# Windowed attention and a rational feed-forward layer: four early halves divided after their value products

## The chip, the cores and the metric

The kernel runs on one core of a Trainium2 chip. The metric is the device time of one execution, in microseconds (us). The engines meant by the short names of the profile are: PE, the matrix engine (PEld is its weight load); DVE, the vector engine; ACT, the scalar engine; POOL, the GpSimd engine; SP, which here only starts transfers. PE accumulates into PSUM, a small memory of banks of 128x512 float32; the other tiles lie in SBUF.

## What is computed

```python
# q, k, v: (4, 8, 768, 64); block 32, window 16, 24 blocks
k_sum = k.reshape(B, H, nb, block, D).max(axis=3)
v_sum = v.reshape(B, H, nb, block, D).mean(axis=3)
scores_l = where(|i - j| < 16, scale * q @ k.T, -1e9)
scores_s = scale * q @ k_sum.T + log(32)
s = concat([scores_l, scores_s]);  a = exp(s - max(s))
a = a / (sum(a) + 1e-9)
attn = a @ concat([v, v_sum])
# x = attn as (3072 tokens, 512)
h = x @ w_in                                  # 512 -> 2048
P = a0 + a1*h + a2*h**2 + a3*h**3
Q = 1 + |b0|*|h| + |b1|*h**2
out = (P / (Q + 1e-6)) @ w_out                # 2048 -> 512
```

## The kernel before

The 3072 tokens are worked in six groups of 512. A group is eight **halves** of 64 query rows; a half `jj` holds all eight heads, as four pairs. One half sees 96 neighbouring keys and 24 block keys, 120 columns for each pair, so that its scores are a tile of 128 rows by 4 x 120. The feed-forward layer walks over 16 slices of 128 hidden columns for each group; a step is `h0` to `h95` (first layer, 12 matmuls of 128x512), the rational function (`gelu`, named so in the code), and `P3` to `P98` (second layer).

The first 16 halves go through `early_half`. Half by half it is a chain of steps on different engines: DVE takes the maximum of each row of scores; ACT forms the exponentials (`ss`); the row sums give a reciprocal (`sm`); the exponentials are multiplied by it; PE transposes them (`pt`), they are copied to SBUF (`pts`), PE multiplies them with the values (`av`); the result is rounded to `xh`, and DVE forms the rest `xl = av - xh`. Together `xh` and `xl` of eight halves are the input of the first layer: `h0` needs all of halves 0 to 7. `PATH` has a letter for each half. Path `B` subtracts the maximum on DVE, takes one exponential over all four pairs, and sums on DVE. Path `A` multiplies the maximum by the scale on DVE and gives it to ACT as a bias, one exponential for each pair, whose row sum ACT gives as well (an extra instruction, `ACTIVATION_READ_ACCUMULATOR`). The division is four multiplications on POOL, or on DVE for the halves in `SSV`.

The block means of the values of the first batch are made by PE (`vs`, ten times four matmuls that read all value tiles), copied by ACT to half 0's value tile and from there to the seven others (`m0` to `m7`). No `av` can run before its half's means are there.

Weights come packed. `w_split` unpacks a slice in up to six steps, and `MODE` has a letter for each slice: in mode `c` ACT forms the high part and DVE subtracts it from the whole to get the low part (`wearly<-wr,wearly`); in mode `e` ACT forms the high part and its negative, and a DMA started by POOL adds the whole onto it.

The order of all this is written out. `ORDER` is a list of 1,698 tokens; each runs one step of one chain (`a3` is the next step of half 3, `h0` the first-layer matmuls of step 0, `w5` the next step of slice 5), and the class `Kept` ties every instruction of an engine behind the one issued before it. So each engine works strictly in the order of the list. `SLOTS` assigns each tile of a pool to one of its buffers, and a tile waits for the readers of the buffer's last tile. `BYDVE` names the copies that DVE makes in place of ACT: `C` is the copy of a half's transposed tile, `X` its rounding to `xh`.

In the profile all of these instructions stand under line 162, the line of `Kept`; they are told apart by tile names.

Of the kernel before, what the change touches and what calls it, by code (L numbers as in the profile page):

```python
# [51 lines left out]
PATH = 'BAAAAAAAAAAAAABB'  # L52
BYDVE = 'C2 C3 C4 C6 X0 X2 X3'
MEANS = 'aaaggggg'
XP = ()
SSV = (3, 5)
AFF = (28,)
FILL = {}
SLOTS = {'wm': '1010', 'ta': '01101010101010101010101010101010101010101010101010101010101010101010101010101010101010101101010101', 'tq': '01010101010101010101010101101010101011001010101010101101010101010101011010010101010101010010101010', 'st': '010101010101010101010101', 'gh': '012020120120120120120120120120120120120120120120121021021021021021021021020120120120120120120210210210', 'h': '0101011110101010101010101010101010010110100100101010101011010101001010101001001010110010101011010110101100101010100101010', 'ks': '0101', 'o': '01230130213021301320132013201320132013201', 'gl': '0121021021021021021021021021021021021021021021021021021021021021021021021021021021021021012102102102', 'sm': '012302312031203102310213021301230132103210321023', 'p': '0132103210123012301021302020232132302103013201021212131032010213013010121321202301021310101013020301021302130', 'xl': '0101010', 'a': '010010101001010101110010101010010111010000010010010111100001101111010010001010011011101000100010101010010100010101010101010101010', 'tu': '010101010101010101010101010101010101010101010101010101010101010101010101010101010101010101101010101', 'xh': '0110101', 'pts': '010101011011011010101011010101010101011011010101', 'vs': '01'}
NROW = 96  # L60
PTP = 'hhhhhhhhaaaaaaaa'
AVP = 'ooooooooaaaaaaaa'
# [10 lines left out]
h3 W8 a9 g2 g1 q2 a8 a9 A10 h4 a8 w6 W7 g2 w6 g1 g1 w6 o a8 a9 D10 L13 a8 P3 w6 w6 a8 g2 g2 g1 a9 g3 w8 g2 w6 g4 V10 W9 a9 q3 g3 w8 g3 b5 w7 q3 a11 P4
a11 w9 w7 q4 g4 g3 g3 W10 g3 q4 g4 a10 D13 a11 h5 w7 P5 w9 a10 L11 g4 h6 w8 g5 g4 w8 L12 w10 w7 g4 P6 w9 P7 D11 V11 q5 A13 D12 q5 g6 g5 w9 w10 w7 a10
a11 w7 g5 a10 g6 w8 h7 q6 a11 A12 g5 w9 a11 k13 a10 a10 a11 g5 a11 a10 a10 w8 g6 k12 w9 a11 W11 a10 q6 b6 g5 w10 g6 g6 g7 g7 W12 q7 w11 w10 w10 g6 g7
q7 a13 a13 A14 h8 A15 g7 g8 w12 a12 w11 P8 g7 h9 g8 w12 q8 w10 g7 w11 w11 q8 w12 g9 P9 W15 g9 g8 P10 a12 g8 h10 g8 w12 g8 w11 b7 a12 g9 q9 w11 q9 g9
w12 g10 W13 g9 P11 a15 h11 w12 V12 g9 w15 q10 a15 W14 a13 g10 P12 w13 a12 w13 g10 a13 V13 a14 q10 g10 A17 h12 g11 g11 w13 a13 g10 q11 w13 w13 g11 a12
w14 q11 g10 a15 a13 P13 w13 a14 w14 g11 a12 g12 g11 g11 a13 a13 g12 V15 q12 a13 a15 g12 h13 g13 P14 a14 w14 q12 a15 g13 w14 g12 a15 a14 a12 a14 w14
w14 g12 h14 q13 a12 a14 a12 a15 q13 V14 g12 w15 g14 a14 a15 a14 g13 w15 a15 w15 w15 P15 A16 a14 q14 g14 w15 g13 b8 q14 A18 g13 a17 g14 g13 h15 A19 a17
g14 g14 g15 g15 g15 q15 a16 q15 h16 P16 g14 g16 g15 a16 g15 g16 P17 h17 q16 L21 g15 P18 q16 g16 g16 g17 f0 a17 g16 q17 g16 a17 f0 g17 a16 g17 q17 g17  # L80
f0 h18 h19 b9 g18 g18 g17 g17 D21 f0 L22 V16 a16 P19 a19 g18 q18 g19 q18 g18 g18 q19 g19 g19 q19 g18 P20 h20 a16 A21 g20 P21 g19 h21 g20 g19 g20 q20
V17 q20 a17 g19 g20 g20 g21 q21 P22 g21 g20 a18 A20 h22 g21 g22 q21 a18 g21 q22 a16 P23 h23 g22 g21 b10 g21 a18 a18 q22 a19 a17 g22 A23 a20 z8 g23 a18
g22 a19 z8 a20 P24 h24 a19 g22 a18 g23 g22 g23 L20 V18 q23 q23 g23 h25 a20 a19 A22 P25 g24 a20 g23 a21 q24 V19 q24 g23 z8 P26 g25 z8 h26 D22 g24 a21
q25 a19 g25 q25 L23 g24 b11 z9 g24 a21 g24 a20 g25 a23 g24 P27 g25 a23 z9 h27 a22 a21 g26 g25 g25 g26 a23 z9 g26 V20 V21 a23 g27 q26 q26 a21 P28 h28
# [34 lines left out]
def tile_kernel(ctx, tc, qw_in, kraw, kwin, vpad, vred, wio, a, b, cmask, cident, cavg, chot, cbias, out):  # L119
# [203 lines left out]
    def early_half(jj):  # L323
# [29 lines left out]
        if path == "B":  # L353
            dve.tensor_reduce(sm[:, 1, :], ss, axis=AX.X, op=ALU.add)
            dve.tensor_scalar_add(sm[:, 1, :], sm[:, 1, :], 1e-9)
# [409 lines left out]
```

## Time and profile before

| | us |
|---|---|
| median of 3 runs (lowest to highest) | 633.54 (632.42 to 634.58) |
| the profiled execution: its time | 634.05 |
| its span in the trace | 632.1 |
| PE busy in the span | 613.5 |
| DVE busy | 558.3 |
| ACT busy | 453.6 |
| POOL busy | 249.5 |

The span is what the trace covers; the 1.95 us beside it are the start and end of the execution. PE is busy nearly all the time from 100 us on; before that several engines wait for one another, and the first transfers run at the limit of the queues. An idle gap is shown by the profile in square brackets behind the instruction that ended it, with the engine or transfer that was waited for.

### The profile page before, as it was taken

To read this page: it belongs to the slowest core of one execution; us is meant where nothing else is said; L and a number is where in the kernel's file an instruction comes from. 1 tells how busy PE (TensorE), PEld (TensorE's weight loads), DVE (VectorE), ACT (ScalarE), POOL (GpSimd) and SP (SyncE) were. 2 spreads that over 40 slices of the span, in tenths; PEclk is the share of its full clock that TensorE was granted. 3 is DMA by queue.
4 is the path that set the end of the run, shared out by engine and by line. 5 is a ranking of instruction groups with operands and counts; after the bars stand their busy time and mean duration, and the time that the engine had idled before them with its cause. 6 is when DMAs were issued, how large, how long until landed. Compare 5 with 4: busy or idle time off the path is not lost.

```text
span 632.1 us, 12059 instructions
## 1 busy us (share of the span) xinstructions
PE 613.5 (97%) x4188; PEld 492.6 (78%) x4188; DVE 558.3 (88%) x1073; ACT 453.6 (72%) x1007; POOL 249.5 (39%) x350
## 2 busy tenths in 40 slices
PE   8689989999999999999999999999999999999997
PEld 4477768777888888888888888887888888888885
DVE  5889999999888999989998799998978987798795
ACT  2898979877678767775876777777865875765653
POOL 0865465752416424224433233344242352122231
PEclk9599999999999999999999999999999999999999
DMA  8999668712334343334463413244423022100001
GB/s 317 268 335 319 234 207 275 183 47 68 105 118 147 121 138 91 120 99 146 114 200 114 156 49 113 82 136 125 136 80 101 26 84 87 67 0 2 0 1 66
DMA packets 52660, 80.25 MB, mean 127 GB/s; under 512 B 6440, under 2 KB 33736, under 8 KB 50680
## 3 DMA queue, kind: packets, MB, share of 16 engines
q1 hardware_dynamic: 51096, 75.00, 37.4%
q0 software_dynamic: 1280, 4.39, 3.0%
q8 instruction: 33, 0.54, 0.4%
q14 instruction: 27, 0.22, 0.1%
q10 hardware_dynamic: 224, 0.09, 0.1%
HBM read 60.33 MB, written 14.75 MB: 119 GB/s over the span
## 4 chain that ended last, share of the span: by engine, by line
PE 73%; DVE 12%; DMA 5%; ACT 4%; issue 2%; POOL 2%; SPq 1%; POOLq 0%; DVEq 0%; ACTq 0%
PE h L162 33%; PE po L162 33%; DVE tu L162 3%; DVE tq L162 3%; PE sc L162 3%; PE av L162 3%; DMA wr<-in_wio_dram 2%; DMA vr<-in_vpad_dram 2%; ACT ta L162 2%; DVE gh L162 2%; DVE wr L162 1%; POOL ss L162 1%; POOL gl L162 1%; DMA kres<-in_kraw_dram 1%; PE vs L162 1%
## 5 line engine op out<-in xcount | busy, mean ns | idle before, releaser
L162 POOL TENSOR_TENSOR gl<-tu,ta 128x512 fp32r<-128x512 f32 x96 | 132.6, 1382 | 327.5 <-DVE tu L162 221.8
L162 PE MATMUL po<-w,gh 128*128 128x512 f32 x384 | 119.7, 393 | 0.0
L162 PE MATMUL po<-wearly,gh 128*128 128x512 f32 x384 | 119.5, 392 | 0.0
L162 PE MATMUL h<-xh,wearly 128*128 128x512 f32 x384 | 97.1, 392 | 1.3 <-ACT xh L162 1.1
L162 PE MATMUL h<-xh,w 128*128 128x512 f32 x384 | 97.3, 392 | 0.0
L162 POOL TENSOR_SCALAR ss<-ss,sm 128x120 f32<-128x120 f32 x184 | 83.8, 473 | 23.0 <-DVE sm L162 22.3
L162 ACT ACTIVATE ta<-tq,cs 128x512 f32<-128x512 f32 x96 | 69.4, 723 | 31.9 <-DVE tq L162 29.5
L162 DVE SCALAR_TENSOR_TENSOR gh<-tu,cs,ta 128x512 fp32r<-128x512 f32 x96 | 74.8, 782 | 16.2 <-ACT ta L162 12.4
L162 PEld LDWEIGHTS h<-xh,wearly 128*128 128x128 f32 x384 | 71.4, 188 | 17.8 <-DVE tu L162 1.4
L162 PEld LDWEIGHTS h<-xh,w 128*128 128x128 f32 x384 | 71.3, 188 | 16.0 <-DVE tu L162 0.5
L162 PEld LDWEIGHTS po<-wearly,gh 128*128 128x128 f32 x384 | 71.5, 188 | 15.4 <-issue 0.6
L162 PEld LDWEIGHTS po<-w,gh 128*128 128x128 f32 x384 | 71.2, 188 | 15.4 <-issue 0.6
L162 ACT ACTIVATE ta<-h,cs 128x512 f32<-128x512 f32 x95 | 64.8, 682 | 22.1 <-POOL gl L162 21.8
L162 DVE SCALAR_TENSOR_TENSOR tu<-tu,cs,tq 128x512 f32<-128x512 f32 x96 | 74.0, 771 | 3.4
L162 ACT ACTIVATE sq<-h 128x512 f32<-128x512 f32 x72 | 42.0, 583 | 48.4 <-PE h L162 32.3
L162 PE MATMUL po<-wearly,gl 128*128 128x512 f32 x192 | 75.1, 391 | 0.6 <-POOL gl L162 0.6
L162 PE MATMUL po<-w,gl 128*128 128x512 f32 x192 | 75.2, 392 | 0.3 <-POOL gl L162 0.2
L162 ACT ACTIVATE tu<-h,cs 128x512 f32<-128x512 f32 x96 | 74.6, 777 | 0.0
L162 DVE SCALAR_TENSOR_TENSOR tu<-tu,cs,h 128x512 f32<-128x512 f32 x96 | 71.2, 743 | 1.8
L162 DVE SCALAR_TENSOR_TENSOR tq<-tq,gh 128x512 f32<-128x512 f32 x96 | 69.9, 729 | 1.8
L162 DVE TENSOR_TENSOR tu<-tu,h 128x512 f32<-128x512 f32 x96 | 65.1, 678 | 5.3 <-ACT tu L162 5.3
L162 ACT ACTIVATE ta<-ta 128x512 f32<-128x512 f32 x96 | 60.8, 634 | 3.0
(99 smaller groups left out, 903.6 us busy)
## 6 DMA issues: line engine op xcount, KB each, us to landing
wr<-in_wio_dram SPq DMA_DIRECT2D x15, 1024.0 KB, 5.5
cross<-tb SPq DMA_DIRECT2D x32, 256.0 KB, 2.1
vw<-in_vpad_dram SPq DMA_DIRECT2D x42, 192.0 KB, 2.8
kw<-in_kwin_dram SPq DMA_DIRECT2D x40, 192.0 KB, 3.3
out_dram<-o SPq DMA_DIRECT2D x24, 256.0 KB, 2.6
pts<-cross SPq DMA_DIRECT2D x96, 64.0 KB, 2.6
qw<-in_qw_dram SPq DMA_DIRECT2D x40, 128.0 KB, 2.9
kr<-in_kraw_dram SPq DMA_DIRECT2D x12, 384.0 KB, 4.3
```

Source lines behind the costliest of these rows:

```text
L162: out = getattr(self.engine, name)(*args, **kw)
```

## The change

- `PATH` goes from `BAAAAAAAAAAAAABB` to `BNANANANAAAAAABB`: halves 1, 3, 5 and 7 take the new path `N`. Its exponentials are formed without row sums. POOL writes 1e-9 into a 121st column of each pair, and the transposes take that column along. Behind the value product PE multiplies the transposed tile with a tile of ones (two matmuls of 256 columns), which puts each query's sum beside its products in the same bank. DVE then takes the reciprocal of those sums (128x256, out of PSUM) and multiplies the products by it; `xh` and `xl` come from that product, which lies in SBUF.
- In paths `A` and `N` the maximum is written into the free end of the scores' own PSUM bank, and the scale is applied on the way from there to SBUF. Before, both were in SBUF.
- Halves 3 and 5 were the ones that DVE divided (`SSV`); with path `N` that branch has no half left.
- `MODE` changes for three slices: 6 and 7 from `c` to `e`, and 12 from `e` to the new `p` (POOL subtracts, in place of the negative on ACT and the DMA).
- `BYDVE` gains `X13`; `AVP` puts the products of half 2 into bank kind `h` and those of half 4 into `a`.
- `ORDER` and `SLOTS` are new, for all engines.

```diff
-PATH = 'BAAAAAAAAAAAAABB'
-BYDVE = 'C2 C3 C4 C6 X0 X2 X3'
+PATH = 'BNANANANAAAAAABB'
+BYDVE = 'C2 C3 C4 C6 X0 X13 X2 X3'
-AVP = 'ooooooooaaaaaaaa'
+AVP = 'oohoaoooaaaaaaaa'
-K1 K0 K3 d1 S d0 K2 d2 B Q0 d3 c Q1 b0 a1 a0 a1 b2 k8 a0 W0 a2 b1 a2 w0 W1 V2 a1
+K1 K3 S K0 d3 Q0 d0 d1 K2 Q1 W1 W0 d2 b0 W2 a0 a1 b2 a0 V2 k9 a1 a2 b1 k8 a2 a1
...
-MODE = 'ccgcacccbceheccc'
+MODE = 'ccgcaceebcehpccc'
+    ones = const.tile([P, D], F32, name="ones")
...
-            dve.tensor_reduce(sm[:, 0, :], flat, axis=AX.X, op=ALU.max, negate=True)
-            if path == "A":
-                dve.tensor_scalar_mul(sm[:, 0, :], sm[:, 0, :], SCALE)
+            peak = sc[:, NPAIR * NK:NPAIR * (NK + 1)] if path in "AN" else sm[:, 0, :]
+            dve.tensor_reduce(peak, flat, axis=AX.X, op=ALU.max, negate=True)
+            if path in "AN":
+                dve.tensor_scalar_mul(sm[:, 0, :], peak, SCALE)
...
+        elif path == "N":
+            for pr in range(NPAIR):
+                act.activation(ss[:, pr, :], flat[:, pr, :], AF.Exp, scale=SCALE, bias=sm[:, 0, pr:pr + 1])
...
+        if later:
+            gps.memset(full[:, :, NK:nk], 1e-9)
+            yield
...
+        total = av[:, NPAIR * HQ:2 * NPAIR * HQ]
         av = av[:, 0:NPAIR * HQ].rearrange("p (r q) -> p r q", r=NPAIR)
+        if later:
+            for e in range(2):
+                pe.matmul(total[e * D:(e + 1) * D, :], ones[0:nk, :],
+                          pts[:, :, (e ^ turn[jj]) * HQ:((e ^ turn[jj]) + 1) * HQ], start=True, stop=True)
+            yield
+            flat = full.rearrange("p r k -> p (r k)")
+            dve.reciprocal(flat[:, 0:NPAIR * HQ], total)
+            of, av = av, flat[:, NPAIR * HQ:2 * NPAIR * HQ].rearrange("p (r q) -> p r q", r=NPAIR)
+            dve.tensor_tensor(av, of, flat[:, 0:NPAIR * HQ].rearrange("p (r q) -> p r q", r=NPAIR), op=ALU.mult)
+        yield
         (dve.tensor_copy if f"X{jj}" in by_dve else act.copy)(xh[:, :, cols], av)
```

Where the list moves instructions, two places matter. The first is DVE between the value means and `h0`. Before the change, from half 3's rounding on (`av3`, `xh0`, `xl0` are the products and the two parts of the first group's input, `pts6` the copy of half 6's transposed tile, `wr3` the unpacking of slice 3):

```order
L162 CAST xh0_517<-av3_559 128x4x64
L162 TENSOR_TENSOR xl0_518<-av3_559,xh0_517 128x4x64
L162 COPY pts6_637<-pt6_487 120x512
L162 TENSOR_TENSOR xl0_518<-av1_574,xh0_517 128x4x64
L162 CAST xh0_517<-av2_622 128x4x64
L162 TENSOR_TENSOR xl0_518<-av4_599,xh0_517 128x4x64
L162 SCALAR_TENSOR_TENSOR wr3_549<-wr3_549 128x1024
```

After it, DVE from the same place on (`ss3`, `ss5` and `ss1` now also hold the reciprocals and products of those halves, `sm8` is the row statistic of half 8):

```order
L163 RECIPROCAL ss3_292<-av3_536 128x256
L163 TENSOR_TENSOR ss3_292<-av3_536,ss3_292 128x256
L163 CAST xh0_494<-ss3_292 128x4x64
L163 COPY pts4_572<-pt4_553 120x512
L163 TENSOR_TENSOR xl0_495<-ss3_292,xh0_494 128x4x64
L163 RECIPROCAL sm8_550<-sm8_550 128x4
L163 COPY pts6_618<-pt6_585 120x512
L163 RECIPROCAL ss5_387<-av5_574 128x256
L163 TENSOR_TENSOR ss5_387<-av5_574,ss5_387 128x256
L163 RECIPROCAL ss1_191<-av1_603 128x256
L163 TENSOR_TENSOR ss1_191<-av1_603,ss1_191 128x256
L163 CAST xh0_494<-av2_623 128x4x64
```

Two instructions have come in for each of the halves 3, 5, 1 and, eight rows further on, 7: a reciprocal of 128x256 and a product; they stand in the one queue in which half 2's `xh`, the unpacking of slice 3 and all later `xl` wait behind them.

The second place is PE in the same stretch. Before the change, from half 3's products to `h0` (`vr`, `vw` and `vlast` are value tiles):

```order
L162 MATMUL av3_559<-pts3_415,vr1_117 64x64 x8
L162 MATMUL av1_574<-pts1_509,vw1_103 64x64 x8
L162 MATMUL pt5_583<-ident_92,ss5_389 120x128 x4
L162 MATMUL av4_599<-pts4_572,vr2_118 64x64 x8
L162 MATMUL av2_622<-pts2_407,vr0_116 64x64 x8
L162 MATMUL pt7_632<-ident_92,ss7_464 120x128 x4
L162 MATMUL av6_644<-pts6_637,vlast_120 64x64 x8
L162 MATMUL av5_661<-pts5_612,vr3_119 64x64 x8
L162 MATMUL av7_679<-pts7_656,vlast_120 64x64 x8
L162 MATMUL h0_0_695<-xh0_517,wearly_105 128x512 x8
```

After it, from half 5's products to the last row ahead of `h0`:

```order
L163 MATMUL av5_574<-pts5_510,vr3_120 64x64 x8
L163 MATMUL av5_574<-pts5_510,ones_107 64x256 x2
L163 MATMUL pt6_585<-ident_92,ss6_404 120x128 x4
L163 MATMUL av1_603<-pts1_372,vw1_103 64x64 x8
L163 MATMUL av1_603<-pts1_372,ones_107 64x256 x2
L163 MATMUL av2_623<-pts2_479,vr0_117 64x64 x8
L163 MATMUL pt7_634<-ident_92,ss7_505 121x128 x4
L163 MATMUL av6_646<-pts6_618,vlast_121 64x64 x8
L163 MATMUL av7_656<-pts7_642,vlast_121 64x64 x8
L163 MATMUL av7_656<-pts7_642,ones_107 64x256 x2
L163 MATMUL av4_679<-pts4_572,vr2_119 64x64 x8
L163 MATMUL pt8_696<-ident_92,ss8_549 120x128 x4
```

The pairs of matmuls with `ones` are new (half 3's stand just ahead of this piece), and the transposes of half 8 (`pt8`), which stood behind the matmuls of `h2` before, now stand ahead of `h0`.

## Rows read from the trace of the kernel before

**Rows 1.** The page: the span, and busy time, share and instructions of each engine

```profile
span 632.1 us, 12059 instructions
PE 613.5 (97%) x4188; PEld 492.6 (78%) x4188; DVE 558.3 (88%) x1073; ACT 453.6 (72%) x1007; POOL 249.5 (39%) x350
```

**Rows 2.** Windows: length, busy (x) of PE, PEld, DVE, ACT, POOL; clock, DMA

```profile
31.98:42.58 10.60, 8.99 (x182) 7.14 (x182) 9.46 (x20) 10.31 (x27) 8.90 (x13) 1.00 1.01 392
42.58:100.00 57.42, 53.25 (x383) 41.74 (x384) 56.13 (x83) 50.26 (x107) 31.44 (x34) 1.00 0.78 253
...
200.00:600.00 400.00, 399.71 (x2507) 326.69 (x2506) 354.82 (x712) 283.22 (x626) 141.13 (x209) 1.00 0.32 97
```

**Rows 3.** Timeline of PE: start, duration, what [idle before, releaser]

```profile
34.03 1.05 PE L162 MATMUL sc<-kw,qw 64*64 64x120 f32 x32
...
36.11 0.64 PE L162 MATMUL av<-pts,vw 120*64 120x64 f32 x16
...
42.58 2.14 PE L162 MATMUL h<-xh,wearly 128*128 128x512 f32 x8 [1.14 <-ACT xh L162]
...
57.43 0.62 PE L162 MATMUL pt<-ident,ss 128*120 128x128 f32 x4 [1.00 <-DVE tq L162]
...
91.27 0.69 PE L162 MATMUL sc<-bias,hot 96*128 96x480 bf16 x2 [1.22 <-DVE xl L162]
```

**Rows 4.** The chain that ended last, 14 to 33 us: start, duration, what

```profile
14.52 12.37 DMA vr<-in_vpad_dram
...
27.02 2.11 PE vs L162 x32
29.13 1.04 PE pt L162 x4
30.17 1.83 PE vs L162 x48
...
32.02 0.25 ACT vw L162
```

**Rows 5.** Timeline of DVE, 37.9 to 41 us

```profile
37.87 0.68 DVE L162 COPY pts<-pt 120x512 f32<-120x512 f32 x1
38.47 0.41 DVE L162 TENSOR_TENSOR xl<-av,xh 128x256 fp32r<-128x256 f32 x1
38.80 0.42 DVE L162 CAST xh<-av 128x256 fp32r<-128x256 f32 x1
39.13 0.42 DVE L162 TENSOR_TENSOR xl<-av,xh 128x256 fp32r<-128x256 f32 x1
39.46 1.22 DVE L162 SCALAR_TENSOR_TENSOR wr<-wr 128x1024 int32<-128x1024 int32 x1
40.59 0.65 DVE L162 TENSOR_REDUCE sm<-sc 128x4 f32<-128x480 f32 x1
```

**Rows 6.** The tile sm: duration of one instruction, min/median/max in ns

```profile
L162 DVE RECIPROCAL sm<-sm x48: 158/171/179, 15.7 to 517.5; 128x4 f32<-128x4 f32 x48
...
L162 DVE TENSOR_SCALAR sm<-sm x16: 170/268/980, 12.7 to 130.4; 128x4 f32<-128x4 f32 x16
```

**Rows 7.** Groups of DVE by shape: busy us, mean ns of one

```profile
L162 DVE TENSOR_TENSOR wearly<-wr,wearly 128x1024 fp32r<-128x1024 f32 x7 | 8.6, 1227 | 0.0
...
L162 DVE TENSOR_SCALAR cs<-cs 128x1 f32<-128x1 f32 x2 | 0.3, 154 | 0.1
```

**Rows 8.** Windows as in rows 2, around the fall and rise of PE's clock

```profile
16.00:17.00 1.00, 0.15 (x12) 0.04 (x4) 0.93 (x4) 1.00 (x7) 1.00 (x4) 1.00 1.04 303
17.00:18.00 1.00, 0.00 (x0) 0.00 (x0) 0.97 (x4) 0.97 (x4) 0.45 (x2) 0.52 1.09 296
...
30.00:31.00 1.00, 1.00 (x25) 0.83 (x24) 1.00 (x3) 0.81 (x2) 1.00 (x2) 0.65 1.05 345
```

**Rows 9.** Timelines of DVE and POOL at one scaling of a maximum

```profile
67.08 2.67 POOL L162 TENSOR_SCALAR wr<-wr 128x1024 int32<-128x1024 uint8 x2
...
68.80 0.98 DVE L162 TENSOR_SCALAR sm<-sm 128x4 f32<-128x4 f32 x1
```

More of the change, by code (lines that the diff above doesn't have):

```diff
@@ L73 @@
[L73 to L84, printed above, removed]
@@ L113 @@
+h89 g88 g87 h90 g89 g88 g88 g89 q89 g90 q89 P90 g89 h91 q90 g89 g89 g89 q90 g91 g90 q91 P91 g90 g91 g90 g90 q91 g90 h92 g91 P92 g91 g91 g92 g92 g91
+q92 q92 h93 g92 g92 g93 P93 g92 g92 q93 h94 q93 h95 g93 g93 g93 g93 g94 P94 g94 q94 g94 g93 g95 P95 P96 q94 g94 g94 g94 g95 q95 g95 q95 g95 g95 g95
+P97 P98 f5 f5 f5 f5
 """
-MODE = 'ccgcacccbceheccc'
+MODE = 'ccgcaceebcehpccc'
 NHALF = NT // HQ
@@ L329, in early_half @@
         pool, tag = (gp, "gl") if early and jj % 2 else (pp, "p")
-        ss = pool.tile([P, NPAIR, P], F32, tag=tag, name=f"ss{jj}")[:, :, 0:NK]
+        full = pool.tile([P, NPAIR, P], F32, tag=tag, name=f"ss{jj}")
+        ss, later = full[:, :, 0:NK], path in "NM"
+        nk = NK + 1 if later else NK
         sm = sp.tile([P, 2, NPAIR], F32, tag="sm", name=f"sm{jj}")
@@ L352, in early_half @@
         yield
-        if path == "B":
-            dve.tensor_reduce(sm[:, 1, :], ss, axis=AX.X, op=ALU.add)
-            dve.tensor_scalar_add(sm[:, 1, :], sm[:, 1, :], 1e-9)
-        dve.reciprocal(sm[:, 1, :], sm[:, 1, :])
-        yield
-        for pr in range(NPAIR):
-            (dve if jj in SSV else gps).tensor_scalar(ss[:, pr, :], ss[:, pr, :], sm[:, 1, pr:pr + 1], 1.0, op0=ALU.mult, op1=ALU.mult)
-        yield
+        if later:
+            gps.memset(full[:, :, NK:nk], 1e-9)
+            yield
+        else:
+            if path == "B":
+                dve.tensor_reduce(sm[:, 1, :], ss, axis=AX.X, op=ALU.add)
+                dve.tensor_scalar_add(sm[:, 1, :], sm[:, 1, :], 1e-9)
+            dve.reciprocal(sm[:, 1, :], sm[:, 1, :])
+            yield
+            if jj in SSV:
+                dve.tensor_tensor(ss, ss, sm[:, 1, :].unsqueeze(2).broadcast_to((P, NPAIR, NK)), op=ALU.mult)
+            else:
+                for pr in range(NPAIR):
+                    gps.tensor_scalar(ss[:, pr, :], ss[:, pr, :], sm[:, 1, pr:pr + 1], 1.0, op0=ALU.mult, op1=ALU.mult)
+            yield
         pt = banks[PTP[jj]].tile([P, 512], F32, tag=PTP[jj], name=f"pt{jj}")
@@ L363, in early_half @@
         for pr in range(NPAIR):
-            pe.transpose(out=pt[:NK, pr * P:(pr + 1) * P], in_=ss[:, pr, :], identity=ident)
+            pe.transpose(out=pt[:nk, pr * P:(pr + 1) * P], in_=full[:, pr, 0:nk], identity=ident)
         yield
         pool, tag = ((mp, "tu") if jj % 5 in (1, 3) else (gp, "gh")) if early else (pp, "p")
-        pts = pool.tile([NK, NPAIR, P], F32, tag=tag, name=f"pts{jj}")
-        (dve.tensor_copy if f"C{jj}" in by_dve else act.copy)(pts, pt[:NK, :].rearrange("k (r q) -> k r q", r=NPAIR))
+        pts = pool.tile([nk, NPAIR, P], F32, tag=tag, name=f"pts{jj}")
+        (dve.tensor_copy if f"C{jj}" in by_dve else act.copy)(pts, pt[:nk, :].rearrange("k (r q) -> k r q", r=NPAIR))
         yield
@@ L380, in early_half @@
                     vt[:, (2 * pr + e) * D:(2 * pr + e + 1) * D],
-                    pts[:, pr, (e ^ turn[jj]) * HQ:((e ^ turn[jj]) + 1) * HQ], start=True, stop=True)
+                    pts[0:NK, pr, (e ^ turn[jj]) * HQ:((e ^ turn[jj]) + 1) * HQ], start=True, stop=True)
+        total = av[:, NPAIR * HQ:2 * NPAIR * HQ]
+        av = av[:, 0:NPAIR * HQ].rearrange("p (r q) -> p r q", r=NPAIR)
+        if later:
+            for e in range(2):
+                pe.matmul(total[e * D:(e + 1) * D, :], ones[0:nk, :],
+                          pts[:, :, (e ^ turn[jj]) * HQ:((e ^ turn[jj]) + 1) * HQ], start=True, stop=True)
+            yield
+            flat = full.rearrange("p r k -> p (r k)")
+            dve.reciprocal(flat[:, 0:NPAIR * HQ], total)
+            of, av = av, flat[:, NPAIR * HQ:2 * NPAIR * HQ].rearrange("p (r q) -> p r q", r=NPAIR)
+            dve.tensor_tensor(av, of, flat[:, 0:NPAIR * HQ].rearrange("p (r q) -> p r q", r=NPAIR), op=ALU.mult)
         yield
-        av = av[:, 0:NPAIR * HQ].rearrange("p (r q) -> p r q", r=NPAIR)
         (dve.tensor_copy if f"X{jj}" in by_dve else act.copy)(xh[:, :, cols], av)
         yield
-        dve.tensor_tensor(xl[:, :, cols], av, xh[:, :, cols], op=ALU.subtract)
+        (gps if later and jj in XLP else dve).tensor_tensor(xl[:, :, cols], av, xh[:, :, cols], op=ALU.subtract)
     def parts(g):
@@ L497, in w_split @@
         for s, w, h32, l32, byte in cooked if wio.dtype != F32 else ():
-            dve.scalar_tensor_tensor(out=h32 if mode in "cd" else packed, in0=h32, scalar=3, in1=l32,
+            dve.scalar_tensor_tensor(out=h32 if mode in "cdp" else packed, in0=h32, scalar=3, in1=l32,
                                      op0=ALU.logical_shift_left, op1=ALU.bitwise_or)
@@ L507, in w_split @@
         wt = weights(fc)
-        whole = [(s, w) for s, w, *_ in cooked] if mode in "cd" else [(slice(0, 2), packed.bitcast(F32))]
+        whole = [(s, w) for s, w, *_ in cooked] if mode in "cdp" else [(slice(0, 2), packed.bitcast(F32))]
         for s, w in whole:
-            if mode in "cef":
+            if mode in "cefp":
                 act.copy(wt[:, 0, s], w)
@@ L522, in w_split @@
         for s, w in whole:
-            if mode in "cda":
-                dve.tensor_tensor(wt[:, 1, s], w, wt[:, 0, s], op=ALU.subtract)
+            if mode in "cdap":
+                (gps if mode == "p" else dve).tensor_tensor(wt[:, 1, s], w, wt[:, 0, s], op=ALU.subtract)
             else:
@@ L604, in tile_kernel @@
     vres += [vlast[:, 0], vlast[:, 1]]
+    if set(PATH) & set("NM"):
+        nc.gpsimd.memset(ones, 1.0)
     zero = gp.tile([P, 512], F32, tag="gh", name="zero")
@@ L672, in tile_kernel @@
         elif kind in "vn":
-            b, total = (0, HPG + 2) if kind == "v" else (1, NJ // 2)
-            if b not in seen:
-                seen[b] = banks[VSP[b]].tile([P, 512], F32, tag=VSP[b], name=f"vs{b}"), 0
-            av, i = seen[b]
-            value_average(av, i, *(fv[1][n] if b else half_rows(n) if n < HPG else fv[0][n - HPG]), total)
-            seen[b] = av, i + 1
+            batch, total = (0, HPG + 2) if kind == "v" else (1, NJ // 2)
+            if batch not in seen:
+                seen[batch] = banks[VSP[batch]].tile([P, 512], F32, tag=VSP[batch], name=f"vs{batch}"), 0
+            av, i = seen[batch]
+            value_average(av, i, *(fv[1][n] if batch else half_rows(n) if n < HPG else fv[0][n - HPG]), total)
+            seen[batch] = av, i + 1
         elif kind == "m":
```

80 lines of the change are left out of this document (45 added, 35 removed).

## The prediction

> **What bounds the kernel now.** I read the page first: PE is busy 613.5 of 632.1 us, DVE 558.3 [rows 1]. Then the windows, to see where PE is not busy: from 200 to 600 us it lacks 0.3 us, so that there only PE's own work counts; from 42.58 to 100 us it lacks 4.2 us while DVE is busy 56.13 of 57.42; before that it mostly waits [rows 2]. So the time is the start of `h0` at 42.58 us, plus the PE work behind it, plus the gaps up to 100 us. The timeline of PE gives the gaps: five, 4.0 us together, the first of 1.00 us at 57.43 and the last of 1.22 us at 91.27 ending in work of DVE [rows 3]. The reader should see in it that `h0` itself waited 1.14 us for `xh` from ACT.
>
> What sets 42.58 the chain tells: a value tile's transfer lasts until 26.9 us, the `vs` matmuls run from 27.02 to 31.98 with one set of transposes in between, and at 32.02 ACT begins to copy the means [rows 4]. From there to `h0`, 10.60 us, ACT is busy 10.31, DVE 9.46 and PE 8.99 [rows 2]: three engines almost full. Whatever the change adds to one of them in this stretch moves `h0`.
>
> **The means.** The same kinds and numbers of tiles must land ahead of the last value tile before and after, so the transfers give nothing. But the 1.04 us of transposes inside the `vs` matmuls [rows 4] now stand ahead of them, where PE waits anyway. I take the end of `vs` at 31.0 us; the bounds are 30.6 (if transfers end a little earlier) and 32.0 (if the last tile is what counts).
>
> **PE in the stretch.** Added are four pairs of matmuls with `ones`, 512 columns each pair. The eight products of a half are 512 columns too and take 0.64 us [rows 3]; four pairs cost 2.6 us at most. `pt8` comes in ahead of `h0`: 1.04 us for its like at half the clock [rows 4, 8], so about 0.55 at full, which is taken off behind `h0`. With the 8.99 us of before [rows 2] that is 12.1 us from 31.0 on, to 43.1, and with a wait or two about 43.5. It is not what comes last, by the next paragraphs.
>
> **ACT in the stretch.** It loses the row sums of half 7 and gains the exponentials of halves 8 and 9, which ran behind `h0` before. They can lie in its waits for the next term: ACT's last `xh` depends on DVE's last product, so ACT's own sum does not decide.
>
> **DVE in the stretch, the term that decides.** With `vs` at 31.0, four copies of means of 0.25 us begin [rows 4]; half 0's products (0.64) and the scores of halves 8 and 9 (1.05 [rows 3], and about half a us for the two mask matmuls ahead of them) follow to 34.3; and DVE's two maxima of those scores at 0.65 us [rows 5] with two scalings of 0.17 [rows 6] bring it to 36.0. From there its queue is fixed: four reciprocals of 128x256 (R each), four products like an `xl` (0.33 from start to start [rows 5]), two `xh` and three `xl` (0.33 each), two copies (0.60 each), the unpacking of slice 3 (1.13) and one small reciprocal (0.1): 4 x 0.33 + 5 x 0.33 + 1.2 + 1.13 + 0.1 = 5.4, then ACT rounds half 7 (0.4) and `h0` can go. `h0` = 36.0 + 5.4 + 0.4 + 4R = 41.8 + 4R. Queued behind each reciprocal are the `xl` of the other halves and the next reciprocal; PE waits for all of them.
>
> No row shows a reciprocal of 256 columns. The lower bound is that it streams like the rounding of the same 128x256 out of PSUM, 0.42 us [rows 5]. The upper is that all 171 ns of the 128x4 reciprocal [rows 6] are element time, 43 ns each: 11 us. The row nearest is the reciprocal's own: its 171 ns are 17 above the 154 of a one-element scalar operation [rows 6, 7], 5.7 ns for each further element, so 0.154 + 255 x 0.0057 = 1.6 us. I take 1.6, as an estimate. The support is thin: by the longest of the 48, 179 ns, it would be 8.3 ns and 2.3 us, by the shortest, 158 ns, 1.3 ns and 0.5 us, and a multiplication of four elements takes 170 as well [rows 6]. These readings are the first two rivals.
>
> [...]
>
> With R = 1.6, `h0` starts at 41.8 + 6.4 = 48.2, which is 5.6 later than 42.58. Nothing covers it: from 36 to 48 us the path is DVE's queue alone.
>
> **PE's clock at `h0`.** PE would then be through at 43.5 and stand idle for 4.7 us. [...] The gap of 1.22 us at 91.27 cost no clock [rows 2, 3]. [...]
>
> **Behind `h0`.** Off come 0.55 (`pt8`) and part of the gaps. DVE loses two subtractions of 1.23 us (slices 6 and 7 in mode `e` [rows 7]) and the waiting in four scalings of a maximum. One of those took 0.98 us in place of 0.17, ending when POOL's two operations of 67.08 to 69.75 did [rows 9]; a median of 0.27 [rows 6] for three others gives 0.3. Together 2.46 + 0.81 + 0.3 = 3.6 us of DVE work, in a stretch where DVE is full and PE has 4.0 us of gaps. The gaps end at different instructions and not all move, so I take 2.5, with bounds 1.0 and 3.6. ACT's two negatives and POOL's two transfers more for these slices lie under DVE. The subtraction on POOL for slice 12 has no row; POOL is idle more than half the time [rows 1], and slice 12 is not needed before 100 us: nothing.
>
> **The sum.** +5.6 + 1.85 - 0.55 - 2.5 = +4.4 us on the profiled execution's own 634.05 (span 632.1 and 1.95 around it): 638.45. That execution is 0.5 above the median of the runs, so I predict 638.0.
>
> **Rivals.**
> - The reciprocal streams like a copy, R = 0.42. Then DVE ends as PE does: `h0` at about 43.6 by DVE's queue (41.8 + 1.7 = 43.5), no idle long enough for the clock, and +1.0 - 0.55 - 2.5 = -2.0: 631.5, faster; 630.4 if all 3.6 are given back. For it speak the shortest small reciprocal and the four-element multiplication; against it, that a divide would then cost as little as a copy. It decides from R below about 0.9.
> - The reciprocal is slower still, R = 2.3 by its longest row: 41.8 + 9.2 = 51.0, +8.4 + 1.85 - 0.55 - 2.5 = +7.2: 640.7. For it speaks that row; against it, that the other 47 are shorter on the mean by 8 ns. [...]
> - The reciprocal is slow, but little of it shows: DVE's delay leaves all the work of the gaps done by the time that PE comes, 3.6 given back and no clock lost: +5.6 - 0.55 - 3.6 = +1.5, 635.0, within the noise. Against it: DVE works in one fixed order, so a late `h0` finds no work done ahead.
> - The list places something badly behind 200 us, where PE has 0.3 us of gaps in 400 [rows 2] and every new wait would add in full. I can't price it by a row but by the gaps before 100 us, about 1 us each: +1 to +3 on any case above.
>
> **Chances.** About 1.9 us, 0.3%, is what a measurement of this kernel can tell from no change. Forecast 0.52 (R of 1.2 to 2, slower almost surely); fast reciprocal 0.27 (faster 0.23, the rest within); slower still 0.11; slow but hidden 0.07 (within, or slower); a bad place later 0.03. Together faster 0.24, within 0.3% 0.10, slower 0.66. The forecast alone lies between 635.5 and 640; the range for eight in ten, with the fast case's middle and the slowest case, is 630.8 to 641.
>
> **What would show it.** The rows `RECIPROCAL ss<-av` of 128x256 in the changed profile: 1.6 us each confirms the term, 0.42 the first rival. `h0` at about 48 us, waiting for `xh` with DVE's `ss` ahead of it; the granted clock at 0.5 from about 45 to 52; `vs` ending near 31.0; `TENSOR_SCALAR sm<-sc` near 0.17 us without one of 0.98; the gaps of 42 to 100 us down from 4.0 to 1.5. Wrong it would be above all if DVE's four reciprocals take under a microsecond each.

## The result, and the profile after

The changed kernel takes 640.51 us (median of 4 runs, 638.24 to 642.95) beside 634.06 us for the kernel before (4 runs, 632.42 to 635.82): a ratio of 1.0108, interval 1.0076 to 1.014. Five more runs, beside others of the kernel before (the experiment g1 below), gave 638.80 and a ratio of 1.0084, 1.007 to 1.0098. So it is slower by about 0.8 to 1.1%, as forecast (638.0, slower). The 640.51 lies half a us above the band of 635.5 to 640 that the prediction gave to its own case, and next to the 640.7 of its rival of a still slower reciprocal; the 638.80 lies inside the band. The time alone does not part these two, the reciprocal's own row below does. The profiled execution took 639.55 with a span of 637.8.

The page of the changed kernel, to be set beside [rows 1]:

```profile
span 637.8 us, 12108 instructions
PE 617.5 (97%) x4204; PEld 496.0 (78%) x4204; DVE 561.5 (88%) x1068; ACT 451.1 (71%) x987; POOL 246.6 (39%) x349
```

The whole says little: PE is busy for 4.0 us more in a span that is 5.7 longer. The stretches say more. These are windows of the changed kernel (length; busy us and instructions of PE, PEld, DVE, ACT, POOL; clock; DMA). The first runs from the end of the `vs` matmuls to `h0`, the stretch that was 10.60 us long in [rows 2]:

```profile
29.25:48.06 18.81, 11.62 (x203) 8.30 (x199) 17.83 (x30) 11.61 (x38) 10.13 (x18) 0.92 0.78 278
48.06:100.00 51.94, 50.23 (x334) 39.32 (x334) 49.24 (x71) 46.04 (x82) 26.04 (x30) 0.96 0.80 252
...
200.00:600.00 400.00, 398.78 (x2529) 325.52 (x2528) 354.07 (x713) 282.18 (x626) 139.78 (x213) 1.00 0.33 100
```

In the first, DVE is busy 17.83 of 18.81 us, while PE and ACT have 7 us to spare each. In the second PE lacks 1.71 us where it lacked 4.17. In the third it lacks 1.22 where it lacked 0.29.

The groups of DVE by shape (busy us, mean ns of one) have the row that no trace of before could show, next to the small reciprocal and the scaling of the maxima [rows 6]:

```profile
L163 DVE RECIPROCAL sm<-sm 128x4 f32<-128x4 f32 x44 | 7.5, 169 | 1.2 <-ACT sm L163 1.1
...
L163 DVE RECIPROCAL ss<-av 128x256 f32<-128x256 f32 x4 | 7.0, 1747 | 0.0
...
L163 DVE TENSOR_SCALAR sm<-sc 128x4 f32<-128x4 f32 x13 | 2.1, 162 | 0.5
```

The timeline of DVE (start, duration, what) shows where the four stand, and the CAST between them is the one row of the stretch that is far longer than its like (0.29 us in e1_copy):

```profile
33.98 1.75 DVE L163 RECIPROCAL ss<-av 128x256 f32<-128x256 f32 x1
35.77 0.42 DVE L163 TENSOR_TENSOR ss<-av,ss 128x256 f32<-128x256 f32 x1
36.23 1.05 DVE L163 CAST xh<-ss 128x256 fp32r<-128x256 f32 x1
...
38.78 1.74 DVE L163 RECIPROCAL ss<-av 128x256 f32<-128x256 f32 x1
...
40.90 1.75 DVE L163 RECIPROCAL ss<-av 128x256 f32<-128x256 f32 x1
...
45.28 1.75 DVE L163 RECIPROCAL ss<-av 128x256 f32<-128x256 f32 x1
47.07 0.42 DVE L163 TENSOR_TENSOR ss<-av,ss 128x256 f32<-128x256 f32 x1
```

ACT waits 3.78 us for the last product, and PE 4.98 for ACT; the timelines of ACT and of PE, where `h0` stood at 42.58 [rows 3]:

```profile
29.35 1.09 ACT L163 COPY vw<-vs 24x128 f32<-24x128 f32 x4 [1.36 <-PE vs L163]
...
47.60 0.40 ACT L163 CAST xh<-ss 128x256 fp32r<-128x256 f32 x1 [3.78 <-DVE ss L163]
```

```profile
48.06 3.78 PE L163 MATMUL h<-xh,wearly 128*128 128x512 f32 x8 [4.98 <-ACT xh L163]
51.64 1.21 PE L163 MATMUL h<-xl,wearly 128*128 128x512 f32 x4
...
82.14 0.50 PE L163 MATMUL po<-wearly,gl 128*128 128x512 f32 x1 [1.30 <-POOL gl L163]
...
100.59 1.19 PE L163 MATMUL h<-xh,w 128*128 128x512 f32 x4 [0.57 <-DMA w<-wr]
```

`h0`'s eight matmuls take 3.78 us where they took 2.14: the granted clock is 0.50 from 46 to 51 us. Windows of one us, the last number but two is the clock:

```profile
44.00:45.00 1.00, 0.00 (x0) 0.00 (x0) 1.00 (x2) 0.00 (x0) 0.00 (x0) 1.00 0.16 61
45.00:46.00 1.00, 0.00 (x0) 0.00 (x0) 1.00 (x3) 0.00 (x0) 0.00 (x0) 0.54 0.00 0
...
51.00:52.00 1.00, 1.00 (x4) 0.77 (x4) 1.00 (x2) 0.00 (x0) 0.60 (x1) 0.55 0.00 0
52.00:53.00 1.00, 1.00 (x6) 0.83 (x5) 0.23 (x1) 0.12 (x1) 0.02 (x1) 1.00 0.49 176
```

One thing must be read beside these times. ACT's copy of the means starts when the last value tile has landed and been multiplied: at 29.35 here, at 32.02 in the profile of before [rows 4]. Over the nine profiles of the new list it starts at 29.35 to 31.09 (mean 30.0), over the four of the old list at 29.73 to 32.02 (mean 30.9). It moves with the transfers from one execution to the next, and `h0` with it. So below, `h0` is also given from that copy: 10.56 us behind it before, 18.71 after. Counted so, the change costs 8.15 us ahead of `h0`; in these two profiles the earlier copy took 2.67 of that off, on the mean of all profiles it takes 0.9.

### The profile page after: what moved, and what is told of

The parts are those of the page before. It is cut to its first block, busy times and chain, and to the rows that moved or that the text cites. A ratio compares the mean times of both kernels' runs of the same rounds, so it can differ in the third digit from the quotient of the medians.

```text
span 637.8 us, 12108 instructions
## 1 busy us (share of the span) xinstructions
PE 617.5 (97%) x4204; PEld 496.0 (78%) x4204; DVE 561.5 (88%) x1068; ACT 451.1 (71%) x987; POOL 246.6 (39%) x349
## 4 chain that ended last, share of the span: by engine, by line
PE 75%; DVE 9%; ACT 4%; DMA 4%; SPq 3%; issue 2%; POOL 2%; POOLq 0%; DVEq 0%; ACTq 0%
PE h L163 34%; PE po L163 33%; PE sc L163 3%; PE av L163 3%; SPq L163 3%; DVE tu L163 2%; DVE tq L163 2%; DVE ss L163 2%; ACT ta L163 1%; PE warm L163 1%; DMA kw<-in_kwin_dram 1%; POOL gl L163 1%; DVE gh L163 1%; DMA w<-wr 1%; DMA wr<-in_wio_dram 1%
## 5 line engine op out<-in xcount | busy, mean ns | idle before, releaser
L163 PE MATMUL h<-xh,wearly 128*128 128x512 f32 x384 | 99.0, 398 | 5.5 <-ACT xh L163 5.0
L163 DVE SCALAR_TENSOR_TENSOR gh<-tu,cs,ta 128x512 fp32r<-128x512 f32 x96 | 78.6, 819 | 14.6 <-ACT ta L163 10.6
L163 POOL TENSOR_SCALAR ss<-ss,sm 128x120 f32<-128x120 f32 x176 | 78.5, 467 | 25.3 <-DVE sm L163 20.2
L163 DVE SCALAR_TENSOR_TENSOR tu<-tu,cs,tq 128x512 f32<-128x512 f32 x96 | 72.2, 752 | 3.4
```

The lines of the kernel that those rows point to most:

```text
L163: out = getattr(self.engine, name)(*args, **kw)
```

## The experiments

The theory: four reciprocals of 1.75 us in DVE's one queue hold `h0` back, and PE's idle time ahead of it costs the clock on top; what DVE is relieved of behind `h0` gives part of it back. The main rivals: the new list costs in other places; the work behind `h0` waits in any case. Each kernel was timed in five rounds beside the kernel before. A difference between one of them and g1 below is uncertain by 1.3 to 2.1 us.

**e1_copy.** A copy in place of each reciprocal: the division is left out, the products are multiplied by their sums.

```
-            dve.reciprocal(flat[:, 0:NPAIR * HQ], total)
+            dve.tensor_copy(flat[:, 0:NPAIR * HQ], total)
```

> The changed kernel with each of the four wide reciprocals replaced by a plain copy of the same 128x256 values out of PSUM; the four halves are then multiplied by their sums instead of divided, all else as in the changed kernel. Theory (four reciprocals of 1.75 us in DVE's queue hold h0 back, and PE's idle time before it costs the clock): a copy takes 0.42, 4 x 1.33 = 5.3 us leave the path, h0 starts near 43 instead of 48.06, the granted clock stays at 1.0 through h0, and the time is 633.5 (632 to 635), a ratio of about 0.999 to the kernel before. Rival (the new list of engines costs in other places, behind 100 us or by the matmuls with ones): h0 comes early, but the time stays at 636 to 639. Second rival (DVE is the bound behind h0 too, so an early h0 only waits later): h0 near 43, the gaps of 50 to 100 us grow from 1.7 to 4 or more, 636 or more.

Measured: 632.98 us, ratio 0.9978 (0.9952 to 1.0004). Against g1's 1.0084 that is 6.7 us. The timelines of its DVE and PE, and its window from `h0` to 100 us:

```profile
34.77 0.41 DVE L163 COPY ss<-av 128x256 f32<-128x256 f32 x1
35.22 0.42 DVE L163 TENSOR_TENSOR ss<-av,ss 128x256 f32<-128x256 f32 x1
35.68 0.29 DVE L163 CAST xh<-ss 128x256 fp32r<-128x256 f32 x1
```

```profile
42.91 2.14 PE L163 MATMUL h<-xh,wearly 128*128 128x512 f32 x8 [0.49 <-ACT xh L163]
```

```profile
42.91:100.00 57.09, 53.95 (x385) 41.94 (x385) 55.25 (x81) 50.27 (x88) 28.22 (x32) 1.00 0.80 262
```

`h0` starts 12.78 us behind the copy of the means, 5.9 less than 18.71, at the full clock: 5.3 are the four reciprocals, and nearly all the rest is the CAST, 0.29 us here instead of 1.05. The theory gave 633.5 and its first rival at least 636: the loss is the reciprocals' duration and what follows from it. The list and the matmuls with `ones`, which this kernel has too, cost no time on balance, though 12.78 is still 2.2 more than the 10.56 of before. A part of the second rival is there: its PE lacks 3.1 us from `h0` to 100 instead of 1.7, and still the time is the theory's.

**e2_fill and e2b_fill20.** PE is kept busy ahead of `h0`, with 30 and with 20 matmuls on the identity.

```
-FILL = {}
+FILL = {'h0': 20}
```

> The changed kernel with 30 more matmuls of 128x128 in front of h0, on the identity and into the bank that h0 then overwrites; they need nothing that h0 waits for, and fill PE's idle time of 4.98 us (30 x 0.145 = 4.4 us). Theory (the clock fell because PE was idle, and h0 at half the clock loses time): h0 starts at 48 as before, its eight matmuls take 2.14 us in place of 3.78, the granted clock is 1.0 in 48 to 52, and the time falls by 1.5 us (1.2 to 1.9) to 639.0. Rival (the work behind h0 waits for DVE and ACT in any case): the clock is back and the time stays at 640.5. Second rival (what costs is PE's idle time alone and the clock falls for another reason): h0 at half clock again, 640.5.

> As e2_fill, with 20 matmuls on the identity instead of 30: each is two instructions of 0.114 us, so that the 30 took 6.86 us and ran 1.8 us into h0's place; 20 take 4.6, from 43.2 to 47.8. Theory (the idle time costs the clock, and half a clock at h0 costs 1.8 us): h0 starts at 48.1 at the full clock, its matmuls end 1.8 us earlier than in the changed kernel, and the time is 638.7 (638.0 to 639.3), ratio 1.0078. Rival (what is behind h0 waits anyway, and e2_fill's gain of 1.5 us was chance of later gaps): 640.0 to 641.

Measured: e2_fill 638.98 us, ratio 1.007 (1.0047 to 1.0094); e2b_fill20 637.38, 1.0047 (1.0028 to 1.0066). In e2_fill the filling ran until 49.82, too long: `h0` started 20.15 us behind the means, which took most of what the clock gave back. Its time came as expected (against g1 it is 0.9 us less), but its expectation was wrong on where `h0` starts. The timeline of PE in e2b:

```profile
44.56 4.63 PE L163 MATMUL h<-ident 128*128 128x128 f32 x40
49.71 2.11 PE L163 MATMUL h<-xh,wearly 128*128 128x512 f32 x8 [0.52 <-ACT xh L163]
51.66 1.07 PE L163 MATMUL h<-xl,wearly 128*128 128x512 f32 x4
52.56 1.07 PE L163 MATMUL h<-xh,wearly 128*128 128x512 f32 x4
```

`h0` starts 18.83 us behind the means, as in the changed kernel (18.71). Its twelve matmuls are through in 52.56 - 49.71 = 2.85 us; in the changed kernel it is 52.68 - 48.06 = 4.62, the next `h` starting at 52.68. The difference, 1.77, is the price of the clock. The time against g1 is 0.37% or 2.3 us less, with some 1.5 us of uncertainty; 1.8 was expected. The 637.38 itself is under the expected 638.0 to 639.3, which had been counted from the 640.5 of four runs. The rival, that the work behind waits in any case, falls.

**e3_ln_exp.** The reciprocal on ACT.

```
-            dve.reciprocal(flat[:, 0:NPAIR * HQ], total)
+            act.activation(flat[:, 0:NPAIR * HQ], total, AF.Ln)
+            act.activation(flat[:, 0:NPAIR * HQ], flat[:, 0:NPAIR * HQ], AF.Exp, scale=-1.0)
```

> The changed kernel with each wide reciprocal on ACT instead of DVE, as the exponential of minus the logarithm (two passes over 128x256 of about 0.38 us each). Theory: DVE loses 7.0 us in the stretch that ends in h0, ACT gains 8 x 0.38 = 3.0 in a stretch where it was idle for 1.6 and 3.8 us; h0 starts at 43 to 44.5 and the time is 633.5 (632 to 635.5). Rival: ACT works in a fixed order too, its passes wait for the sums and hold up the copies and roundings behind them, and h0 comes at 46 or later: 636 to 639.

Measured: 636.83 us, ratio 1.0055 (1.0028 to 1.0081): the rival. The timelines of its ACT and PE:

```profile
34.40 0.39 ACT L163 ACTIVATE ss<-av 128x256 f32<-128x256 f32 x1 [2.10 <-POOL vr L163]
34.82 0.42 ACT L163 ACTIVATE ss<-ss 128x256 f32<-128x256 f32 x1
...
42.62 0.57 ACT L163 COPY pts<-pt 121x512 f32<-121x512 f32 x1
```

```profile
43.24 1.12 PE L163 MATMUL av<-pts,vlast 120*64 120x64 f32 x16 [1.97 <-ACT pts L163]
...
47.35 2.91 PE L163 MATMUL h<-xh,wearly 128*128 128x512 f32 x8 [0.24 <-ACT xh L163]
```

The first logarithm starts after a wait of 2.10 us (its sums leave PE at 33.97), and the exponentials of halves 8 and 9 stand behind it in ACT's order. A copy of transposed exponentials (`pts`) that PE needs comes at 42.62 instead of 40.28; PE waits 1.97 us for it, and the clock falls again (0.59 over 45 to 50 us, and 2.91 us for the eight matmuls). `h0` is 17.40 us behind the means. The work was cheap on ACT, its place was not.

**p_n135.** One wide reciprocal fewer: half 7 takes the old path.

```
-PATH = 'BNANANANAAAAAABB'
+PATH = 'BNANANAAAAAAAABB'
```

> The changed kernel and its list with half 7 on the old path (row sums with the exponentials on ACT, a small reciprocal, the scaling of the weights on POOL): three wide reciprocals instead of four, the one that stands last before h0 being gone. Theory (each wide reciprocal with its product is 2.1 us of DVE's queue ahead of h0): DVE is through 2.1 us earlier, half 7's own longer chain (POOL's 1.4, the transposes, the copy) ends at about the same time, h0 starts 16.5 to 17 us behind the end of vs instead of 18.9, still at half the clock, and the time is 638.4 (637.5 to 639.3), ratio 1.007. Rival (the longer chain of half 7 comes last in its place): h0 18.9 or more behind vs, 640.5 or more.

Measured: 637.28 us, ratio 1.0064 (1.005 to 1.0079), 1.3 us under g1, as much as the uncertainty, where 2.1 was expected; 637.28 is just under the expected 637.5 to 639.3. The timeline of PE:

```profile
41.70 1.49 PE L163 MATMUL pt<-ident,ss 128*120 128x128 f32 x4 [3.05 <-POOL ss L163]
...
46.79 2.08 PE L163 MATMUL h<-xh,wearly 128*128 128x512 f32 x8
```

`h0` is 17.38 us behind the means, 1.3 earlier and not 2.1: half 7's transposes wait 3.05 us for POOL, which is the rival's chain. In the list the half's small reciprocal, which POOL needs, stands on DVE behind half 5's wide one, and from 35 to 45 us DVE is busy for 9.83 us and POOL for 5.62: it is DVE's queue again, by another way. Against what was expected, `h0`, with PE at work from 41.70 on, had the full clock: 1.00 from 46.79 to 100 us, after 0.87 over 35 to 45. The gaps up to 100 us are 2.56 instead of 1.71.

**e4_modes.** The two subtractions back on DVE, in the new list.

```
-MODE = 'ccgcaceebcehpccc'
+MODE = 'ccgcacccbcehpccc'
```

> The changed kernel and its list, with slices 6 and 7 in mode c again: two subtractions of 1.23 us come back to DVE, ACT's negatives and POOL's two adding transfers for them go. Theory (the prediction's gain behind h0 comes from DVE being relieved of these): PE's gaps in 55 to 100 us grow by 1.5 to 2.5 and the time is 642.5 (641.5 to 643.5). Rival (the gain came with the order of the new list, and DVE has the 2.46 us to spare there): 640.5. Second rival (the list has the subtraction's place too late, and slice 6 or 7 comes late to its first use): 644 or more.

Measured: 644.19 us, ratio 1.0149 (1.0119 to 1.0178), 4.1 us over g1. The timeline of PE:

```profile
34.08 1.88 PE L163 MATMUL sc<-kw,qw 64*64 64x120 f32 x32
...
86.50 0.50 PE L163 MATMUL po<-wearly,gl 128*128 128x512 f32 x1 [2.71 <-POOL gl L163]
...
93.30 0.50 PE L163 MATMUL po<-wearly,gl 128*128 128x512 f32 x1 [1.04 <-POOL gl L163]
```

The gap of 1.30 us at 82.14 became 2.71, and one of 1.04 is new: 2.45 us, as much as the two subtractions of 1.23 that DVE has again. This is the theory's term. Its `h0` also started 20.08 us behind the means instead of 18.71, ahead of which the modes change nothing. There PE had waited 1.75 us for a value tile and then worked at a lower clock, 0.67 over 25 to 35 us and 0.87 over 35 to 45, where the changed kernel had 0.85 and 1.00: the scores took 1.88 us instead of 1.05, and DVE was busy for 6.36 us from 25 to 35 instead of 9.09. As far as the profile shows this comes of the late tile of that execution, not of the modes. The time alone (over the 643.5 of the theory, in the second rival's reach) would not decide. No wait for a late slice is among its gaps from `h0` to 112 us.

**e5_peak_sbuf.** The maxima back in SBUF, in the new list.

```
-            peak = sc[:, NPAIR * NK:NPAIR * (NK + 1)] if path in "AN" else sm[:, 0, :]
+            peak = sm[:, 0, :]
```

> The changed kernel with the maxima back in SBUF: they are reduced into sm and scaled from there, as in the kernel before; nothing else differs. Theory: the 13 scalings, 162 ns each out of PSUM, become some 0.3 us each on the mean with one or two near 1 us where POOL works beside them, 1 to 2 us of DVE in all, of which the part in the full stretches shows: 641.2 (640.5 to 642). Rival (the maxima's place matters to no wait of PE): 640.5, and the scalings stay at 0.17.

Measured: 643.82 us, ratio 1.015 (1.0123 to 1.0177), 4.2 us over g1, more than expected. The timelines of DVE, of POOL and of PE, and two windows:

```profile
76.50 0.65 DVE L163 TENSOR_REDUCE sm<-sc 128x4 f32<-128x480 f32 x1
77.18 0.95 DVE L163 TENSOR_SCALAR sm<-sm 128x4 f32<-128x4 f32 x1
```

```profile
75.74 2.37 POOL L163 TENSOR_SCALAR wr<-wr 128x1024 int32<-128x1024 uint8 x2
```

```profile
84.02 0.70 PE L163 MATMUL po<-wearly,gl 128*128 128x512 f32 x1 [2.11 <-POOL gl L163]
```

```profile
83.00:84.00 1.00, 0.00 (x0) 0.00 (x0) 1.00 (x2) 0.97 (x2) 1.00 (x2) 1.00 0.83 292
84.00:85.00 1.00, 0.98 (x3) 0.79 (x4) 0.97 (x3) 1.00 (x3) 0.80 (x1) 0.57 1.02 367
85.00:86.00 1.00, 1.00 (x4) 0.81 (x3) 1.00 (x2) 1.00 (x3) 0.00 (x0) 0.50 0.89 311
```

One scaling, begun while POOL works on `wr`, ends with it: 0.95 us instead of 0.16. DVE is full there, and `gl` comes later, so that PE's gap of 1.30 becomes 2.11, by 0.8 us. Behind that gap the clock is at half until about 87.5, which costs 3.5 / 2 = 1.8 us. So 0.8 us of delay cost 2.6. The rest up to 4.2 is not placed; it is less than the uncertainty of 1.9 us.

**f3_before_both, f4_before_peak6, f1_before_peak.** The parts that relieve DVE, put into the old list without the wide reciprocals: the maxima in PSUM (all three), with slices 6 and 7 in mode `e` (f3), slice 6 alone (f4), neither (f1).

```
-            dve.tensor_reduce(sm[:, 0, :], flat, axis=AX.X, op=ALU.max, negate=True)
+            peak = sc[:, NPAIR * NK:NPAIR * (NK + 1)] if path == "A" else sm[:, 0, :]
+            dve.tensor_reduce(peak, flat, axis=AX.X, op=ALU.max, negate=True)
...
-MODE = 'ccgcacccbceheccc'
+MODE = 'ccgcaceebceheccc'
```

> The kernel before, with its own list, and only the two parts of the change that relieve DVE: the maxima of the divided-early halves stay in PSUM and are scaled from there, and slices 6 and 7 take mode e (the subtraction leaves DVE). Theory (the prediction's term of the gaps behind h0): DVE loses 2.46 + 0.8 + 0.3 us of work, the gaps of PE in 42 to 100 us fall from 4.0 to about 1.5, h0 stays near 42.5, and the time is 631.5 (630.4 to 633), ratio 0.996. Rival (the gaps close only because the new list orders the work in another way): 634, ratio 1.000, the gaps still near 4. Second rival (ACT's two negatives and POOL's two transfers now come last): 635 or more.

> The kernel before and its list, with the maxima scaled out of PSUM and slice 6 alone in mode e; slice 7 stays in mode c, since in f3_before_both its adding transfer, issued at 85.0 us behind ACT's negative, held h7 back for 4.05 us and h8 for 2.7. Theory (f3 lost its time at slice 7 alone): h7 and h8 wait for no transfer, the gaps up to 80 us fall from 2.7 to 1.2 as they did in f3, DVE is relieved of 1.23 + 0.8 + 0.3 us, and the time is 632.3 (631 to 633.5), ratio 0.997. Rival (the gain is swallowed by DVE's next full stretch): 634, ratio 1.000.

> The kernel before and its list, with the maxima scaled out of PSUM and nothing else changed (f4_before_peak6 without slice 6's new mode). Theory (in f4 both parts give their own DVE time back: about 0.8 to 1.1 us of scalings, 1.23 us of subtraction): 633.1 (632.3 to 633.8), ratio 0.999. Rival (the long scaling next to POOL is what all of f4's gain came from): 632.3, ratio 0.9978. Second rival (the place of the maxima changes nothing in this list): 633.9.

Measured: f3 641.22 us, ratio 1.0104 (1.0067 to 1.0141); f4 632.27, 0.9978 (0.996 to 0.9996); f1 632.78, 0.9982 (0.9962 to 1.0002). In f3 the second rival won. PE's waits from 42 to 110 us (us in total, times, longest) and the timeline:

```profile
PE h L162 <- DMA wearly<-wr: 4.1, 1, 4.1
PE h L162 <- DMA w<-wr: 2.7, 1, 2.7
```

```profile
89.65 1.69 PE L162 MATMUL h<-xh,wearly 128*128 128x512 f32 x4 [4.05 <-DMA wearly<-wr]
```

In mode `e` POOL's adding transfer takes the subtraction's place. Here POOL issued it at 85.04, behind ACT's negative, and it landed 4.6 us later, with `h7` waiting. The new list has slice 7's steps earlier; that this alone lets the mode pay is not tested by itself. f4 leaves slice 7 alone and is under both kernels, though its interval ends only just below 1, with its gaps from `h0` to 100 at 3.64 instead of 4.17 us: that is 0.5 of the 1.4 us of its gain, the rest was not found in the profile. Between f1 and f4 the runs do not decide.

**g1_changed_again.** The changed kernel, unaltered.

> The changed kernel once more, unaltered, beside the next two on one chip: it fixes the ratio that e2b, e4 and e5 are compared with. Theory (the ratio of four runs, 1.0108, is right, and e2b's 1.0047 holds a bit of chance beside the clock's 1.8 us): 1.008 to 1.012, 640.5. Rival (the four runs were low or high): 1.0075 or less, or over 1.0125. The value tiles' landing sets h0: in this execution h0 should start 18.9 us behind the end of vs, as in the changed kernel's first profile.

Measured: 638.80 us, ratio 1.0084 (1.007 to 1.0098), span 636.4; the ratio is within the expected 1.008 to 1.012. `h0` started at 48.04, 18.67 us behind the means. Two of its windows:

```profile
48.04:100.00 51.96, 50.18 (x334) 39.25 (x334) 49.33 (x71) 46.09 (x82) 26.08 (x30) 0.96 0.80 253
...
200.00:600.00 400.00, 399.28 (x2534) 326.47 (x2533) 354.09 (x715) 282.40 (x627) 140.59 (x214) 1.00 0.32 100
```

From `h0` to 100 us it is the first profile over again. Behind 200 it lacks 0.72 us instead of 1.22, which bears on the last step below.

## Why the prediction was right, step by step

**Start of `h0`: +5.6 predicted, 48.06 - 42.58 = +5.48 measured.** The mechanism is the predicted one, but two sizes were off and met by chance. The means came at 29.35 rather than 31.0, which brought DVE to the first reciprocal at 33.98 instead of 36.0. Over all profiles they came at 30.0 on the mean, so part of that gain was this execution's. The way from there to `h0` took 14.1 us instead of 12.2: the reciprocals are 1.79 from start to the next start instead of 1.6, together 0.75 more; the CAST took 0.96 from start to start instead of 0.33; and some 0.5 went into short waits for the result of the instruction just before (half 3's product is 0.46 us from start to start ahead of the CAST that reads it, the other three 0.34 ahead of a row that does not). With the means at 31.0, as it assumed, `h0` would have come at 31.0 + 18.7 = 49.7, 1.5 us behind what it said.

**The wide reciprocal: 1.6 taken, 1.747 measured**, between the estimates from the mean and from the longest small row. The first rival (0.42) is out, and e1 shows that it would have given 633, not 631.5. The second (2.3) is out by the same row. The two shapes give (1747 - 169) / 252 = 6.3 ns for each further element; the 128x4 form, whose 171 ns lie 17 above a one-element operation [rows 6, 7], had hinted at 5.7.

**The clock: +1.85 predicted, 1.77 measured** (e2b against the changed kernel). The 1.85 in the sum was the author's estimate, which no run shows; the runs showed 1.77 in its place. The granted clock fell from 1.00 to 0.50 near 45.0, PE having ended its last matmul at 43.08, and rose near 52.0, PE having worked on `h0` since 48.06. [rows 8] have such a fall and rise in the kernel before.

**Behind `h0`: -2.5 predicted, -2.46 measured, in part by chance.** PE's gaps up to 100 us went from 4.17 to 1.71. e4 shows what they hang on: 2.46 us of subtractions put back bring 2.45 us of gaps. e5 shows the same of a single stalled scaling. The prediction gave the scalings 1.1 us in all; in the new list their place is worth more, since a long one there also costs the clock. But the size rests on the late `h0` too. e1 has the same list and modes with an early `h0`, and its gaps are 3.14, only 1.0 under those of before. Between it and the changed kernel lie 0.57 us of waiting for slice 8 that fall just behind 100 us in the changed kernel, and 0.85 that the late `h0` spared: slice 8 had come nearer to being ready (0.57 of waiting instead of 1.01), and a copy for `av` was done (0.41). So the third rival, that a late `h0` finds work done, holds in small, against the reason given there; and 1.0 instead of 2.5 behind an early `h0` is about why e1 took 633. f3 and f4 limit this step as well: these edits in the old list lose 7 us (f3) or, without slice 7's, gain 1.4 (f4), so the order of the new list has a part in it that no run measures by itself.

**The rest.** `pt8` and the `ones` were not separable from the stretch; e1, which has both, leaves them no loss on balance. A bad place behind 200 us was given a chance of 0.03: PE lacks 1.22 us there where it lacked 0.29, but 0.72 in g1 and 0.79 in e1 with the same list, so some half a us may be lost there, not more than single profiles scatter. From 100 to 600 us it lacks 0.81 + 1.22 = 2.03 us where it lacked 0.95; 0.57 of the 2.03 is the wait for slice 8. The sum 5.48 + 1.77 - 0.55 - 2.46 + 1.08 is 5.3, with `pt8`'s 0.55 as predicted; the span grew by 5.7. Behind 600 us PE lacks 4.32 us instead of 3.76, which covers the 0.4 that is left over.

## What to carry to other kernels

Before moving work to a cheaper engine, ask for the shape in which the rest of it will then be done: the sums cost PE 0.6 us a half, but on PE they come out repeated over 64 rows, and a reciprocal of four elements (0.17 us) became one of 256 (1.75 us) on the engine whose queue set the next stage. Where an idle stretch of PE ends in its slower clock, add what that costs (1.77 us here behind 4.98 of waiting), and try cheap filling work there. An edit that swaps a computation for a transfer is worth what its place in the order allows: price it by when it is issued and when it lands, not by the engine time that it frees.

## What the hardware showed that was not expected

- DVE's reciprocal has a long time for each element, 6.3 ns, next to a copy of the same 128x256 at 0.41 us in all (e1).
- A scaling of four elements took 161 to 163 ns each time out of PSUM (13 of 13), and 170 to 953 out of SBUF (e5); the longest ran beside POOL's work and ended when it did (78.13 and 78.11 us). The CAST that took 1.05 us in the changed kernel also read SBUF; it started at 36.23, during POOL's unpacking of 36.00 to 37.13, and took 0.29 in e1, where that unpacking started behind it. What holds them up there is not shown.
- The clock does not go by the length of a gap alone: after 2.11 us without work it fell to half (e5, 84 us), after 2.71 us it stayed at full (e4, 86.50), as this window of e4 shows:

```profile
86.00:87.00 1.00, 0.50 (x2) 0.46 (x3) 0.96 (x3) 0.97 (x3) 0.45 (x1) 1.00 0.74 258
```
